# Moving the products of one chunk from GpSimd to VectorE, with three smaller changes of order, in a fused attention and FFN kernel

## The chip, the cores and the metric

The kernel runs on one core of a Trainium2 chip. Times are device microseconds (us) of one execution. A profile of one execution gives the "span", which is some 1.7 to 2.1 us shorter than the time, and the granted clock of TensorE. Engines: PE is TensorE, PEld its weight loads, DVE is VectorE, ACT is ScalarE, POOL is GpSimd, SP is SyncE. L392 is line 392 of the kernel profiled; from line 540 on the changed kernel's numbers are 6 or 7 lower than those of the kernel before.

## The reference

Attention with two kinds of local mask, then a gated FFN on its result:

```python
# q, k, v: 8 batches x 8 heads x 576 positions x 64, float32
scores = q @ k.T / 8
rel = pos[:, None] - pos[None, :]
mask_plain = (rel >= 0) & (rel < 32)                       # heads 0 to 3
mask_dil = (rel >= 0) & (rel < 128) & (rel % 4 == 0)       # heads 4 to 7
attn = softmax(where(mask, scores, -1e9)) @ v
x = attn.transpose(0, 2, 1, 3).reshape(4608, 512)
out = (gelu(x @ w_gate) * (x @ w_val)) @ w_out             # 512 -> 1536 -> 512
```

## The kernel before

The 4608 tokens go through the FFN in 9 chunks of 512. A chunk has 12 "ffn blocks" (128 gate and 128 value columns each, 8 matmuls) and then an "output phase" of four token blocks of 12 matmuls. Attention for later tokens is woven into the output phases. It goes by head pairs, numbered through all batches, four to a batch. Per pair: scores on TensorE, exponential on ScalarE, mask product on VectorE, sums and values on TensorE, then the divisors (a VectorE transpose out of PSUM, a reciprocal, a transpose back to `rb`) and the product with them into `xT`, the FFN's input.

In chunk 2 alone two of these products were given to GpSimd. GpSimd got them through a ScalarE copy `xc`:

```python
def norm_x(n, b0, flip=False, split=False):
    ...
        eng = nc.vector
        if split:
            xc = nrm.tile([P, 2, 2 * NCL], F32, tag="xc", bufs=1)
            nc.scalar.copy(xc, ps[:, b0 + flip : b0 + flip + 2, 0 : 2 * NCL])
            eng, num = nc.gpsimd, xc.rearrange("p s (m i) -> p i m s", m=2)
        eng.tensor_tensor(dst..., num, rb..., ALU.mult)
```

A string says where each piece stands in an output phase. "2.3v" means: in token block 2, before matmul 3, sums, values and divisors of the next pair; `s` is the scores of a further pair, `m` its mask product, `x` the product with the divisors on VectorE, `p` the same split over ScalarE and GpSimd, `w` a last pair in two parts.

```python
places = {
    1: "0.0m 1.3v 1.3s 1.3x 1.3m 2.5v 2.5s 2.5x 2.5m 3.0s 3.0m 3.6v 3.6x 3.12w",
    2: "0.0m 1.3v 1.3p 1.3s 1.3m 2.3v 2.3p 2.3s 2.3m 2.11s 3.0m 3.4s 3.5v 3.5x 3.12w 3.12m",
    ...
```

At the start, GpSimd's queue carries the q/k "eights", the last v rows (`vr`), and then the first weights `w0`; SyncE's queue carries the five parts of the v load (`sv`) and the dilated v load. `w0` is issued only when one part of `sv` has landed, the gate.

```python
qd0 = load_eights(0)
sv0 = new_v(0)
load_v_dil_rest(0)                      # vr
... identity and masks on GpSimd ...
gate_v = v_plain(0, sv0, nc.sync)       # returns the second part of sv
...
gate["dma"] = gate_v
load_w(0)
v_cast(0, sv0)
```

The softmax here doesn't subtract the row's maximum and nothing guards it: scores larger than these inputs give would overflow.

## Time and profile before

| | before |
|---|---|
| time, median of 3 | 352.05 us (351.19 to 352.19) |
| span of the profiled run | 350.2 us |
| TensorE busy | 336.9 us, 96% |
| stretch of chunk 2 | 24.06 us, of which TensorE idle 3.05 us |

The "stretch of chunk 2" runs from the first scores woven into its output phase to the second half of the third ffn block of chunk 3. The lines of the order in time are read so: the columns are start, duration, engine, line, operation, out<-in with shapes, and a count where equal neighbours are merged; the bracket tells how long the engine stood before it and what released it. This line, of the kernel before, ends the stretch:

```profile
144.78 0.59 PE L582 MATMUL ps<-xT,wv 128*128 128x512 f16 x2 [0.54 <-DVE u_all L605]
```

TensorE stood 0.54 us for a VectorE product of the first ffn blocks.

### The profile page before, as it was taken

Reading aid. Unit: us, or ns where it says so; the run is one execution under the profiler, and the core shown is the slowest. Engines: PE = TensorE matmul, PEld = TensorE weight load, DVE = VectorE, ACT = ScalarE, POOL = GpSimd, SP = SyncE. Lnnn points to the kernel's source line nnn. Section 1 sums busy time; section 2 is a strip of 40 time slices with the busy share of each in tenths; the row PEclk is TensorE's granted clock in tenths of the full one; section 3 lists DMA queues with packets and bytes.
Section 4 is the critical chain, followed back from the end, with each engine's and each line's share of the span. In section 5 each row is a group of like instructions: output and inputs, shape, how many; then the busy total and the mean of one; then the engine's idle time right before and its main releaser. Section 6 shows DMA issues by size and latency. Waiting matters only on the chain.

```text
span 350.2 us, 6012 instructions
## 1 busy us (share of the span) xinstructions
PE 336.9 (96%) x2342; PEld 163.8 (47%) x2342; DVE 202.3 (58%) x306; ACT 149.7 (43%) x223; POOL 86.4 (25%) x123
## 2 busy tenths in 40 slices
PE   8979989999999979999999999999999999999996
PEld 3644454444544444444454454444454444444444
DVE  3784488543793358783878666985399424303320
ACT  1853373435543537325553547326723223322321
POOL 8692404630630635063006300420000000000000
PEclk9999999999999999999999999999999999999999
DMA  8999999999999983999159953890200020021002
GB/s 180 227 197 230 201 184 186 186 160 266 179 149 227 173 157 69 229 151 140 63 156 178 135 112 113 190 151 32 90 2 0 32 90 1 2 79 41 2 30 90
DMA packets 106460, 44.44 MB, mean 127 GB/s; under 512 B 83296, under 2 KB 101856, under 8 KB 106432
## 3 DMA queue, kind: packets, MB, share of 16 engines
q1 hardware_dynamic: 84192, 31.01, 39.4%
q0 software_dynamic: 21696, 12.33, 27.2%
q10 hardware_dynamic: 544, 0.72, 0.8%
q8 instruction: 18, 0.29, 0.4%
q14 instruction: 10, 0.08, 0.1%
HBM read 39.85 MB, written 9.44 MB: 141 GB/s over the span
## 4 chain that ended last, share of the span: by engine, by line
PE 72%; DVE 10%; DMA 10%; issue 3%; ACT 2%; SPq 1%; POOL 1%; DVEq 0%; ACTq 0%; POOLq 0%
PE ps L582 42%; PE ps L616 22%; PE ps L464 4%; DMA st<-in_k_dram 4%; DMA sv<-in_v_dram 3%; DMA wv<-in_moe_w_val_dram 3%; DVE dt L492 2%; DVE u_all L605 2%; DVE P L392 2%; DVE dt L525 1%; DVE xT L502 1%; PE ps L352 1%; PE ps L382 1%; DVE rb L536 1%; PE ps L640 1%
## 5 line engine op out<-in xcount | busy, mean ns | idle before, releaser
L604 ACT ACTIVATE g<-ps 128x512 f16<-128x512 f32 x108 | 63.9, 597 | 123.7 <-PE ps L582 123.2
L605 DVE SCALAR_TENSOR_TENSOR u_all<-g,ps 128x512 f16<-128x512 f16 x108 | 72.8, 684 | 75.9 <-PE ps L582 67.9
L582 PE MATMUL ps<-xT,wv 128*128 128x512 f16 x432 | 113.8, 379 | 1.1 <-DMA wv<-in_moe_w_val_dram 0.6
L582 PE MATMUL ps<-xT,wg 128*128 128x512 f16 x432 | 114.2, 379 | 0.7 <-POOL xT L706 0.4
L616 PE MATMUL ps<-wo,u_all 128*128 128x512 f16 x420 | 97.2, 380 | 0.1
L582 PEld LDWEIGHTS <-wv 128*128 128x128 f16 x432 | 42.3, 98 | 53.4 <-issue 2.1
L582 PEld LDWEIGHTS <-wg 128*128 128x128 f16 x432 | 41.3, 98 | 48.6 <-issue 1.1
L616 PEld LDWEIGHTS <-u_all 128*128 128x128 f16 x420 | 38.4, 98 | 44.3 <-issue 0.7
L627 ACT ACTIVATE osb<-ps 128x512 f32<-128x512 f32 x33 | 19.7, 598 | 39.9 <-PE ps L616 39.9
L220 POOL CAST qp<-st 128x2048 f16<-128x2048 f32 x6 | 11.4, 1895 | 89.4 <-DMA st<-in_k_dram 71.8
L536 DVE STREAM_TRANSPOSE rb<-rc 128x576 f32<-128x576 f32 (+4 forms) x34 | 25.3, 743 | 1.4
L525 DVE STREAM_TRANSPOSE dt<-ps 128x576 f32<-128x576 f32 x21 | 16.4, 779 | 14.4 <-PE ps L464 14.2
L384 ACT ACTIVATE P<-ps 128x1152 f16<-128x1152 f32 x16 | 18.1, 1131 | 11.4 <-PE ps L382 11.1
L362 ACT ACTIVATE P<-ps 128x960 f16<-128x960 f32 x16 | 15.5, 972 | 7.1 <-PE ps L352 7.0
L392 DVE TENSOR_TENSOR P<-P,mask_d 128x1152 f16<-128x1152 f16 x13 | 11.5, 886 | 10.3 <-ACT P L384 10.3
L557 DVE TENSOR_TENSOR xT<-ps,rb 128x576 f16<-128x576 f32 x14 | 15.6, 1128 | 2.1 <-PE ps L464 1.9
L464 PE MATMUL ps<-P,ones 128*64 128x96 f16 (+5 forms) x174 | 11.2, 245 | 3.7 <-DVE P L392 3.3
L392 DVE TENSOR_TENSOR P<-P,mask_p 128x1344 f16<-128x1344 f16 x14 | 12.9, 939 | 3.3 <-ACT P L363 3.3
L464 PEld LDWEIGHTS <-ones 128*64 128x64 f16 x174 | 6.9, 109 | 13.0 <-issue 8.3
L629 DVE TENSOR_SCALAR osb<-ps 128x512 f32<-128x512 f32 x2 | 1.4, 692 | 18.2 <-PE ps L616 18.2
L247 POOL DMA_DIRECT2D vr<-in_v_dram x16 | 9.9, 628 | 7.3 <-DMA wv<-in_moe_w_val_dram 4.6
L204 POOL CAST vp<-sv 128x1024 f16<-128x1024 f32 x8 | 8.5, 1062 | 11.9 <-DMA sv<-in_v_dram 11.9
(88 smaller groups left out, 254.5 us busy)
## 6 DMA issues: line engine op xcount, KB each, us to landing
out_dram<-osb SPq DMA_DIRECT2D x35, 256.0 KB, 2.0
sv<-in_v_dram SPq DMA_DIRECT2D x40, 128.0 KB, 3.7
st<-in_q_dram SPq DMA_DIRECT2D x24, 128.0 KB, 3.7
st<-in_k_dram SPq DMA_DIRECT2D x24, 128.0 KB, 3.1
vd<-in_v_dram POOLq DMA_DIRECT2D x7, 256.0 KB, 7.1
wg<-in_moe_w_gate_dram POOLq DMA_DIRECT2D x3, 512.0 KB, 7.4
wv<-in_moe_w_val_dram POOLq DMA_DIRECT2D x3, 512.0 KB, 9.2
wo<-in_moe_w_out_dram POOLq DMA_DIRECT2D x3, 512.0 KB, 20.8
```

What stands on the lines that cost most here:

```text
L362: nc.scalar.activation(pt[:, :, 0:PB], sb[:, 0, :, 0:PB], AF.Exp, bias=0.0, scale=scale)
L384: nc.scalar.activation(pt, ps[:, b0 : b0 + 4, 0:DW], AF.Exp, bias=0.0, scale=scale)
L392: nc.vector.tensor_tensor(pt, pt, mb, ALU.mult)
L464: nc.tensor.matmul(o, lhs, rhs, start=st, stop=True, skip_group_check=True)
L525: nc.vector.transpose(dst, den)
L536: nc.vector.transpose(rb[:, 0 : 32 * nb].rearrange("p (b c) -> p b c", c=32), bass.AP(tensor=rc.tensor, offset=rc.offset, ap=[rc.ap[0], [1 ...
L557: eng.tensor_tensor(dst.rearrange("p (i m s) -> p i m s", m=2, s=2), num, rb.rearrange("p (s m i) -> p i m s", s=2, m=2), ALU.mult,)
L582: nc.tensor.matmul(ps[:, bank, :], w[:, kc, ns], xT[kc][:, tok], start=first, stop=end)
L604: nc.scalar.activation(g, ps[:, banks[0], :], AF.Gelu)
L605: nc.vector.scalar_tensor_tensor(u_all[:, nb, :], g, USCALE, ps[:, banks[1], :], ALU.mult, ALU.mult)
L616: nc.tensor.matmul(ps[:, bank, :], u_all[:, fc, tb * P : (tb + 1) * P], wo_t[fc // 4][:, fc % 4, :], start=(fc == 0), stop=(fc == NNB - 1),)
L627: nc.scalar.activation(osb, ps[:, bank, :], AF.Copy, bias=0.0, scale=1.0 / USCALE)
```

## The change

The intent: take the two products of chunk 2 back to VectorE and space its pieces as in chunk 1, since the GpSimd products and the VectorE masks got in each other's way; share the first casts differently between VectorE and ScalarE; let `w0` go as soon as the first part of `sv` is there. One mask product of chunk 0 also moves.

```diff
 def v_plain(b, sv, eng):
-            if kb == 1:
-                second = ins
-        return second
+            if kb == 0:
+                first = ins
+        return first
 def norm_x
-            if split: ... ScalarE copy, product on GpSimd ...
 first casts
-    for hp in range(2):
-        for t in range(2):
-            cast_six(("dve", "act")[t], q6, first_p, t, hp)
+    for t, hp, eng in ((0, 0, "dve"), (0, 1, "dve"), (1, 0, "act"), (1, 1, "dve")):
+        cast_six(eng, q6, first_p, t, hp)
 places
-        2: "0.0m 1.3v 1.3p 1.3s 1.3m 2.3v 2.3p 2.3s 2.3m 2.11s 3.0m 3.4s 3.5v 3.5x 3.12w 3.12m",
+        2: "0.0m 1.3v 1.3s 1.3x 1.3m 2.5v 2.5s 2.5x 2.5m 3.0s 3.0m 3.6v 3.6x 3.7s 3.12w 3.12m",
 chunk 0
             third(1, 0)
+            mask_next()
             den(4, 0)
-            mask_next()
```

More of the change, by code (lines that the diff above doesn't have):

```diff
@@ L540, in recip, with norm_x @@
         tiles["rb", n] = rb
-    def norm_x(n, b0, flip=False, split=False):
+    def norm_x(n, b0, flip=False):
         b = n // NHP
@@ L551, in norm_x @@
             num = ps[:, b0 + flip : b0 + flip + 2, 0 : 2 * NCL].rearrange("p s (m i) -> p i m s", m=2)
-            eng = nc.vector
-            if split:
-                xc = nrm.tile([P, 2, 2 * NCL], F32, tag="xc", bufs=1)
-                nc.scalar.copy(xc, ps[:, b0 + flip : b0 + flip + 2, 0 : 2 * NCL])
-                eng, num = nc.gpsimd, xc.rearrange("p s (m i) -> p i m s", m=2)
-            eng.tensor_tensor(
+            nc.vector.tensor_tensor(
                 dst.rearrange("p (i m s) -> p i m s", m=2, s=2),
@@ L868, in do @@
                     mask_next()
-                elif kind in "xp":
-                    norm_x(*going.pop(0), split=kind == "p")
+                elif kind == "x":
+                    norm_x(*going.pop(0))
                 elif kind == "v":
```

## The prediction

In rival (a) the words cut said that the masks' losses, 1.5 and 1.2 us (2.28 against 0.76, 2.86 against 1.65), would go away. No term of the sum is cut; it came to 352.05 - 2.4 - 0.3 - 0 + 0.4 = 349.75. The 2.4 rests on the times of chunk 1 (0.76 us for the mask, 1.13 us for the product). The 0.4 is an estimate from the packets counted in the trace: 157 on GpSimd's queue and 157 on SyncE's from 9 to 10 us, then 208 and 205, and 261 and 269 in the two microseconds after. "Full" in it means that the 16 DMA engines were busy for 90% or more of every slice of 1.5 us from 3 to 51 us.

> **What bounds the kernel now.** First the page: the span, the busy shares and the chain that ended last.
>
> ```profile
> span 350.2 us, 6012 instructions
> ...
> PE 336.9 (96%) x2342; PEld 163.8 (47%) x2342; DVE 202.3 (58%) x306; ACT 149.7 (43%) x223; POOL 86.4 (25%) x123
> ...
> PE 72%; DVE 10%; DMA 10%; issue 3%; ACT 2%; SPq 1%; POOL 1%; DVEq 0%; ACTq 0%; POOLq 0%
> ```
>
> TensorE works nearly throughout, so only places where it stands can give time. A step counts if it moves the moment at which TensorE goes on. I looked next at the stretch from the first scores of a chunk's output phase to the second half of the third ffn block of the next chunk, for chunks 1, 2 and 3.
>
> ```profile
> core 0: us, PE busy (x) PEld busy (x) DVE busy (x) ACT busy (x) POOL busy (x), PEclk, DMA share, GB/s
> 83.31:104.22 20.91, 20.45 (x198) 10.32 (x197) 15.48 (x26) 10.96 (x15) 8.84 (x12) 1.00 1.13 165
> 120.72:144.78 24.06, 21.01 (x204) 10.44 (x204) 17.33 (x26) 13.74 (x20) 7.60 (x8) 1.00 0.79 143
> 161.86:181.73 19.87, 19.67 (x183) 9.78 (x183) 13.79 (x20) 12.31 (x17) 0.73 (x2) 1.00 0.46 104
> ```
>
> Chunk 2 has 3.05 us of idle TensorE (24.06 less 21.01), the others 0.46 and 0.20. Its order of instructions in time says why:
>
> ```profile
> 126.07 0.64 ACT L555 COPY xc<-ps 128x576 f32<-128x576 f32 x1 [1.59 <-DVE dt L525]
> 127.31 2.13 POOL L557 TENSOR_TENSOR xT<-xc,rb 128x576 f16<-128x576 f32 x1 [1.05 <-DVE rb L536]
> 127.78 2.28 DVE L392 TENSOR_TENSOR P<-P,mask_d 128x1152 f16<-128x1152 f16 x1 [0.62 <-ACT P L384]
> 130.11 0.44 PE L464 MATMUL ps<-P,ones 128*64 128x192 f16 x8 [1.90 <-DVE P L392]
> 133.76 2.86 DVE L392 TENSOR_TENSOR P<-P,mask_p 128x1344 f16<-128x1344 f16 x2 [0.90 <-ACT P L363]
> ```
>
> The mask product took 2.28 us; the same form took 0.76 us in chunk 1. It ends 0.62 us after GpSimd's product (127.31 + 2.13 = 129.44). The second GpSimd product stretches the two plain masks to 2.86 us, against 1.65 us in chunk 1. The ScalarE copy also holds the exponential until 126.61, though its scores were finished at 125.51.
>
> The start, where parts two and three act:
>
> ```profile
> 11.93 0.78 POOL L139 DMA_DIRECT2D wg<-in_moe_w_gate_dram  x1 [1.36 <-DMA sv<-in_v_dram]
> 15.04 1.04 POOL L204 CAST vp<-sv 128x1024 f16<-128x1024 f32 x1 [1.59 <-DMA sv<-in_v_dram]
> 18.19 1.06 POOL L293 CAST vd<-st 128x1024 f16<-128x1024 f32 x1
> 20.66 0.38 PE L582 MATMUL ps<-xT,wg 128*128 128x512 f16 x1 [0.37 <-POOL xT L706]
> 21.64 0.39 PE L582 MATMUL ps<-xT,wv 128*128 128x512 f16 x1 [0.60 <-DMA wv<-in_moe_w_val_dram]
> 41.52 0.43 PE L306 MATMUL ps<-ident,qp 96*128 96x96 f16 x6 [0.57 <-POOL qp L293]
> ```
>
> The last line is the key one. TensorE finishes six transposes at about 40.79 (40.53 + 6 x 0.043) and stands until 41.52, for a cast of a k load that landed at 40.6. The DMA engines are full from 2 to 50 us, so whatever TensorE gains earlier than this is lost here, and up to 0.73 us of delay is absorbed here.
>
> [...] The plain product from PSUM takes 0.76 us; the dilated one, with its reordered access, takes 1.13 us, and I use that. [...] From 9 to 10 us, with 1024-byte packets on the GpSimd queue and mostly 256-byte ones on the SyncE queue[...]:
>
> ```profile
> q0 software_dynamic: 157, 0.15, 91.7%
> q1 hardware_dynamic: 157, 0.04, 33.2%
> ```
>
> **Part 1, chunk 2.** Removed: two ScalarE copies (0.64 us) and two GpSimd products (2.13 us). Added: two VectorE products of 1.13 us. Chunk 1 has this schedule already, so I lay its intervals over chunk 2. Nothing moves up to the sums of head pair 12, at 124.43. Scores 13 then end at 125.45, and 14 ffn matmuls (0.216 us each) end at 128.5. VectorE: transposes and reciprocal end at 127.16 as now, product 127.2 to 128.33, mask 13 to about 129.05. So pair 13 starts at 129.1 instead of 130.11: 1.0 us. Chunk 1's intervals then give (offset from pair 13's start): the following mask done 4.7 us later, pair 14 at 133.85. Now it is 136.42, since scores 15 and 16 both stand before it and wait for the exponentials; the change moves scores 16 behind it. From pair 14 the VectorE chain is unchanged: divisors and product 3.5 us, the last pair in two parts 3.4 us, mask 16 0.85 us, the first ffn product 0.65 us. It ends at 142.25 and TensorE's third ffn block goes on at 142.35 instead of 144.78. Gain 2.4 us, with 1.9 to 2.8 possible. Idle left: 0.6 us before pair 13, 0.5 before pair 14, 0.7 before the third ffn block. TensorE runs on from there and the next batch's data land at 129.0 and 163.1, well before their scores (134.8 and about 170), so the gain stays.
>
> **Part 2, chunk 0's masks.** The diff also moves one mask product ahead of a divisor:
>
> ```profile
> 51.16 0.82 DVE L392 TENSOR_TENSOR P<-P,mask_p 128x1344 f16<-128x1344 f16 x1
> 52.02 0.48 PE L464 MATMUL ps<-P,ones 128*64 128x512 f16 x6 [0.58 <-DVE P L392]
> ```
>
> The exponential for that mask is done at 49.14, so it can run 49.2 to 50.0, and the sums start at 51.3 instead of 52.02. VectorE's total there is the same, though: the next divisor's read still ends at 53.4, and the next sums overwrite those banks, so they start at 53.45 instead of 53.77. Gain 0.3 us.
>
> **Part 3, first casts.** ScalarE has two casts of 0.83 us (8.44 to 10.01), VectorE two of 0.60 us (to 8.89). After: ScalarE one, VectorE three, to about 9.45. TensorE's warm-up runs to 9.2 and its 24 transposes follow without a break but for 0.08 us at 9.94, which waited for the second k cast. The bias product moves to 9.95, still before TensorE wants it at 10.3. Gain 0.1 us, then lost at the q/k load of 13.15 that TensorE already waits for, and again at 41.52: 0.
>
> **Part 4, the gate.** The first v part landed at 9.38, the second at 11.64. GpSimd finishes its masks at 10.56, so w0 is issued at about 10.6 instead of 11.93. Can it help? wv landed at 21.60, and TensorE waited at 21.64. But the fourth weight step waits for VectorE's product of pair 3, done at 24.1, and TensorE now stands only 0.1 us there. So earlier weights give nothing behind 24.1. They can hurt: their packets (98 ns each) take turns with the last v parts and the dilated v load on the SyncE queue. w0's packets appear about 2 us after issue, so from about 12.9 instead of 14.3. Between 13 and 16 the SyncE queue must still move about 600 packets of 256 bytes and 500 of 1024. Sharing at the 9-to-10 rate (157 a microsecond, against 563 from 13 to 14 beside only the tail of the other loads) I estimate the cast at 15.04 0.5 to 1 us later and the one at 18.19 1 to 1.5 us later; all that follows on GpSimd slips, and the first ffn block ends 0 to 1.7 us later, 1.1 as a middle. The stop at 41.52 absorbs 0.73. Cost 0.4 us, between 0 and 1.
>
> Sum: 352.05 - 2.4 - 0.3 - 0 + 0.4 = 349.75.
>
> **Rivals.** (a) VectorE becomes the bound in chunk 2, since it gets 2.3 us more while it already carries 17.33 us in the stretch: for it, 0.6 us of new waiting before pair 13; against it, [...]chunk 1 runs this order with 0.46 us idle. It would leave a gain of about 1 us in part 1: 352.05 - 1 - 0.3 + 0.4, so 351.1. (b) The gate costs its full 1.5 us or more, with a hole in the weight queue that moves the load landing at 40.6: 352.05 - 2.7 + 1.5, so 350.9. For it, DMA shares near full; against it, total bytes do not change. (c) The gate costs nothing, as the v loads are nearly through by 13: 349.3, the sum without the 0.4. (d) The gate helps the start: only if the load landing at 40.6 moved forward, against a full DMA: 348.8 with half a microsecond of it.
>
> **Range and chances.** Chunk 2 carries the change; its spread is 0.5 us each way, the start's about 0.5. Runs of the kernel before spread over 1 us. I say 349.7, between 348.7 and 350.9. 2% is 7 us, more than all idle time touched here: within 2% almost surely.
>
> **What would show it.** No ScalarE copy and no GpSimd product in chunk 2, mask 13 at about 0.76 us, pair 13 at 4.65 us after pair 12's start, and the stretch at 21.6 us instead of 24.06. In chunk 0 the wait at 52.02 gone and 0.3 us at most kept. At the start w0's issue at 10.6, the v cast and dilated-v cast later than 15.04 and 18.19, and the wait at 41.52 smaller or gone. I am wrong if the chunk 2 stretch stays above 23 us, if the casts come no later, or if the k load moves from 40.6.

## The result, and the profile after

Four runs of each kernel on one chip: 349.15 us median after (349.05 to 349.6) against 351.66 before (351.19 to 352.19). Ratios in this text are the mean time of one kernel's fast runs over the mean of the other's of the same rounds, so not quite the ratio of the medians quoted; here 0.9931, with a 95% interval of 0.9911 to 0.995. That is 2.4 us, within 2%, and within the range predicted.

The page of the changed kernel:

```profile
span 347.3 us, 6004 instructions
...
PE 335.7 (97%) x2342; PEld 163.3 (47%) x2342; DVE 202.1 (58%) x309; ACT 147.9 (43%) x220; POOL 82.2 (24%) x121
...
PE 71%; DVE 12%; DMA 10%; issue 3%; ACT 2%; POOL 1%; SPq 1%; DVEq 0%; POOLq 0%; ACTq 0%
```

VectorE was given two products more and yet was busy no longer (202.1 against 202.3 us): the products took 1.14 us each, but the masks of pairs 13 to 15 took 2.42 us instead of 5.14, and the page counts all of that as busy. The same three stretches, chunks 1, 2 and 3, with the columns as in the prediction:

```profile
82.73:103.66 20.93, 20.46 (x198) 10.32 (x198) 15.51 (x26) 10.96 (x15) 8.85 (x12) 1.00 1.22 174
120.16:141.88 21.72, 20.50 (x204) 10.46 (x203) 16.80 (x28) 12.33 (x18) 3.08 (x5) 1.00 0.69 135
158.97:178.84 19.87, 19.68 (x184) 9.78 (x184) 13.80 (x20) 12.30 (x17) 0.00 (x0) 1.00 0.48 108
```

Chunk 2 went from 24.06 to 21.72 us, chunks 1 and 3 kept theirs. The order in time in chunk 2:

```profile
126.63 1.14 DVE L551 TENSOR_TENSOR xT<-ps,rb 128x576 f16<-128x576 f32 x1
127.69 0.75 DVE L392 TENSOR_TENSOR P<-P,mask_d 128x1152 f16<-128x1152 f16 x1
128.49 0.44 PE L464 MATMUL ps<-P,ones 128*64 128x192 f16 x8 [0.41 <-DVE P L392]
132.32 1.67 DVE L392 TENSOR_TENSOR P<-P,mask_p 128x1344 f16<-128x1344 f16 x2
133.24 0.49 PE L464 MATMUL ps<-P,ones 128*64 128x64 f16 x10 [0.22 <-DVE P L392]
141.88 1.02 PE L576 MATMUL ps<-xT,wv 128*128 128x512 f16 x4 [0.23 <-DVE u_all L599]
```

The mask of pair 13 takes 0.75 us (before 2.28), the two plain masks 1.67 (before 2.86), and TensorE's wait for the mask of pair 13 falls from 1.90 to 0.41 us. Pair 14 starts 4.75 us after pair 13, with a wait of 0.22 us. The line that ends the stretch waits 0.23 us instead of 0.54.

Chunk 0, where the mask moved:

```profile
49.07 0.86 DVE L392 TENSOR_TENSOR P<-P,mask_p 128x1344 f16<-128x1344 f16 x1 [0.66 <-ACT P L363]
51.27 0.48 PE L464 MATMUL ps<-P,ones 128*64 128x512 f16 x6
```

The sums no longer wait. And the start:

```profile
10.76 0.78 POOL L139 DMA_DIRECT2D wg<-in_moe_w_gate_dram  x1
15.25 1.04 POOL L204 CAST vp<-sv 128x1024 f16<-128x1024 f32 x1 [2.96 <-DMA sv<-in_v_dram]
21.84 0.39 PE L576 MATMUL ps<-xT,wv 128*128 128x512 f16 x1 [0.59 <-DMA wv<-in_moe_w_val_dram]
41.42 0.43 PE L306 MATMUL ps<-ident,qp 96*128 96x96 f16 x6 [0.26 <-POOL qp L293]
```

`w0` is issued 1.17 us earlier (10.76 against 11.93), but the v cast (before 15.04) and TensorE's wait for the value weights (before 21.64) are no earlier.

**Where the 2.9 us of span went.** The kernel can be split at four moments that every profile has. The first is the stop at 41.4 (six transposes that wait for the next batch's k), the second the first ffn matmul of chunk 1, the third the first scores of chunk 2's output phase, the fourth the end of the stretch.

| us | start to the stop | stop to chunk 1 | to chunk 2's scores | stretch of chunk 2 | to the end | span |
|---|---|---|---|---|---|---|
| before | 41.52 | 20.96 | 58.24 | 24.06 | 205.44 | 350.22 |
| after | 41.42 | 20.49 | 58.25 | 21.72 | 205.44 | 347.32 |
| difference | 0.10 | 0.47 | -0.01 | 2.34 | 0 | 2.90 |

In three later profiles (chunk2_back, only_mask, only_casts) the k load had landed by 40.0 us and TensorE passed the stop without a wait, so the stop does not always absorb what happens before it.

So three questions were put to the chip. Does each part do what this table says when it stands alone? What in chunk 2 made the gain: the engine, or the places? And why did an earlier issue of `w0` move nothing?

### The profile page after: what moved, and what is told of

It reads as the page before. It is cut to its first block, busy times and chain, and to the rows that moved or that the text cites. A ratio compares the mean times of both kernels' runs of the same rounds, so it can differ in the third digit from the quotient of the medians.

```text
span 347.3 us, 6004 instructions
## 1 busy us (share of the span) xinstructions
PE 335.7 (97%) x2342; PEld 163.3 (47%) x2342; DVE 202.1 (58%) x309; ACT 147.9 (43%) x220; POOL 82.2 (24%) x121
## 4 chain that ended last, share of the span: by engine, by line
PE 71%; DVE 12%; DMA 10%; issue 3%; ACT 2%; POOL 1%; SPq 1%; DVEq 0%; POOLq 0%; ACTq 0%
PE ps L576 42%; PE ps L610 21%; PE ps L464 4%; DMA st<-in_k_dram 4%; DMA sv<-in_v_dram 3%; DMA wv<-in_moe_w_val_dram 3%; DVE dt L492 2%; DVE u_all L599 2%; DVE dt L525 2%; DVE rb L536 1%; DVE P L392 1%; DVE xT L551 1%; DVE xT L502 1%; PE ps L382 1%; PE ps L352 1%
## 5 line engine op out<-in xcount | busy, mean ns | idle before, releaser
L551 DVE TENSOR_TENSOR xT<-ps,rb 128x576 f16<-128x576 f32 x16 | 17.9, 1131 | 2.2 <-PE ps L464 1.9
L392 DVE TENSOR_TENSOR P<-P,mask_d 128x1152 f16<-128x1152 f16 x13 | 9.8, 750 | 9.7 <-ACT P L384 9.7
L392 DVE TENSOR_TENSOR P<-P,mask_p 128x1344 f16<-128x1344 f16 x14 | 11.8, 856 | 2.9 <-ACT P L363 2.9
L492 DVE STREAM_TRANSPOSE dt<-ps 64x576 f32<-64x576 f32 x14 | 10.9, 781 | 0.4
```

Of the source, the lines that this page charges most:

```text
L392: nc.vector.tensor_tensor(pt, pt, mb, ALU.mult)
L492: nc.vector.transpose(dt[64 * hl : 64 * hl + 64].rearrange("p b c -> p (b c)"), both_rows(1 - hl, b0, hl))
L551: nc.vector.tensor_tensor(dst.rearrange("p (i m s) -> p i m s", m=2, s=2), num, rb.rearrange("p (s m i) -> p i m s", s=2, m=2), ALU.mult,)
```

## The experiments

Each group of runs has its own rounds of the kernel before.

### Each part alone

Kernel before in these rounds: 351.51 us median of 11 runs (350.91 to 353.2).

**chunk2_back**: the changed kernel with the split products and the old places of chunk 2, that is, the other three parts alone.

```diff
+ norm_x with split as before
-        2: "0.0m 1.3v 1.3s 1.3x 1.3m 2.5v 2.5s 2.5x 2.5m 3.0s ... (new)
+        2: "0.0m 1.3v 1.3p 1.3s 1.3m 2.3v 2.3p 2.3s 2.3m 2.11s ... (old)
```

> The changed kernel with chunk 2 alone as it was before (split products on ScalarE and GpSimd, old places). My theory: chunk 2 carries 2.3 to 2.4 us, the rest about 0.5, so this is 0.3 to 0.6 us faster than before (about 351.3 against 351.7 to 352.0) and the stretch from the first scores of chunk 2 to the third ffn block's second half is back at 24.06 us. Rival (the gain is the start's, or the parts help each other): over 1 us faster than before.

**only_mask**: the kernel before with the mask of chunk 0 moved.

```diff
             third(1, 0)
+            mask_next()
             den(4, 0)
-            mask_next()
```

> Before, with only the mask product of chunk 0 moved ahead of the divisor. My theory: the sums that started at 52.02 start at about 51.3, the next ones at 53.2 to 53.5, so 0.3 to 0.6 us faster. Rival: the 0.57 us seen at the end of chunk 0 came from the k load's landing and other chance at the start; then 0.1 us or less here.

**only_gate**: the kernel before with the gate of `w0` on the first part of `sv`.

```diff
-            if kb == 1:
-                second = ins
-        return second
+            if kb == 0:
+                first = ins
+        return first
```

> Before, with only the gate of w0 on the first v part. As I predicted before the change ran: v casts 0.5 to 1.5 us later than 15.04 and 18.19, first ffn block later by about 1 us, 0 to 1 us slower in all. New theory from the changed kernel's trace (w0 lands no earlier though it is issued 1.2 us earlier): w0 issued at about 10.6, landing at 21.6 to 21.8, v casts within 0.3 us of before, total within 0.2 us of before.

**only_casts**: the kernel before with the first casts shared anew.

```diff
-            cast_six(("dve", "act")[t], q6, first_p, t, hp)      # for hp, for t
+    for t, hp, eng in ((0, 0, "dve"), (0, 1, "dve"), (1, 0, "act"), (1, 1, "dve")):
+        cast_six(eng, q6, first_p, t, hp)
```

> Before, with only the three casts on VectorE. Theory: the first scores 0.1 to 0.2 us earlier, nothing left of it at the wait for k's cast near 41.5 us, total within 0.2 us of before. Rival: the start's gain survives, 0.2 us or more faster.

Measured:

| | time, median (range) | ratio to before, 95% | to the stop | stop to chunk 1 | stretch of chunk 2 |
|---|---|---|---|---|---|
| chunk2_back | 351.41 (350.5 to 351.9) | 0.9986 (0.9965 to 1.0007) | 40.84 | 20.48 | 24.05 |
| only_mask | 350.91 (350.06 to 351.89) | 0.9978 (0.9955 to 1.0002) | 40.83 | 20.48 | 23.38 |
| only_gate | 352.32 (351.91 to 353.12) | 1.0017 (0.9996 to 1.0039) | 41.45 | 20.96 | 24.05 |
| only_casts | 352.31 (351.14 to 353.11) | 1.001 (0.9986 to 1.0035) | 40.93 | 20.96 | 25.66 |

None of the four times can be told from the kernel before; all ratio intervals hold 1, so the times neither confirm nor refute the gains of 0.3 to 0.6 us that were expected of chunk2_back and only_mask. One expectation was missed: in only_casts the first scores came at 11.26 us, later than the 10.99 of the kernel before and not 0.1 to 0.2 us earlier. The stages of the table tell more than the times. With the moved mask the interval from the stop to chunk 1 is 20.48 or 20.49 us, without it 20.96; the same holds in every later profile. So this part is worth 0.48 us. The gate and the casts touch neither interval.

The stretch of chunk 2 is another matter: with its old code it took 24.06, 24.05 and 24.05 us, but 23.38 in only_mask and 25.66 in only_casts, and neither edit touches chunk 2. In the order in time of only_mask, GpSimd and VectorE show why:

```profile
126.61 1.23 POOL L260 COPY kTr<-qTd 128x512 f16<-128x512 f16 x1 [4.48 <-DMA qTd<-rd]
126.61 0.76 DVE L392 TENSOR_TENSOR P<-P,mask_d 128x1152 f16<-128x1152 f16 x1 [0.63 <-ACT P L384]
```

Here a copy of keys, which waits for a load, came up on GpSimd just as the mask of pair 13 began. The mask took its short 0.76 us, and the copy took 1.23 us instead of its usual 0.61. GpSimd's product came behind both. In only_casts GpSimd's product is first, by 0.06 us (by 0.47 us in the kernel before, chunk2_back and only_gate), and an earlier mask in the same stretch had already taken 1.38 us instead of 0.76 beside the casts of v on GpSimd:

```profile
127.16 2.12 POOL L557 TENSOR_TENSOR xT<-xc,rb 128x576 f16<-128x576 f32 x1
127.22 2.69 DVE L392 TENSOR_TENSOR P<-P,mask_d 128x1152 f16<-128x1152 f16 x1 [0.62 <-ACT P L384]
```

That is only the first 0.4 of the 1.6 us that only_casts lost in this stretch (25.66 against 24.06). TensorE stood 2.30 us for the mask of pair 13 there, against 1.90 in the kernel before, chunk2_back and only_gate. Then, from 130.22 to 133.64 us, the granted clock was 0.50, which the stretch of no other profile here shows:

```profile
129.96 0.48 PE L464 MATMUL ps<-P,ones 128*64 128x192 f16 x8 [2.30 <-DVE P L392]
131.55 2.91 PE L616 MATMUL ps<-wo,u_all 128*128 128x512 f16 x8
```

The eight output matmuls of the last line took 1.90 us in the kernel before. Some 0.8 us more was lost by the end of the half clock, and the last 0.4 us at the third ffn block, behind a gap of 0.47 us on VectorE whose cause the trace does not show. That the longer wait brought the half clock on is not shown: it is one profile, and no run varied the wait alone.

So the old chunk 2 was not just slow but uneven: which of the two engines started first differed between these profiles, and in only_mask it was a copy waiting for a load until 126.61 us that put GpSimd's product last. With VectorE's products at the new places it took 21.72 in three profiles (after, and two runs below). The spread of the times agrees: the kernel before ranges over 2.3 us in these rounds, the changed kernel over 0.55 us in its four runs. Part of that spread goes with the clock: of the 53 runs of the experiments that had the old code of chunk 2, 13 have a mean clock of 0.994 or 0.995 and a median of 352.91 us, the other 40 one of 351.56. None of the 36 runs with any other code of chunk 2 is under 0.998.

### What in chunk 2 made the gain

Kernel before in these rounds: 351.91 us median of 7 runs (351.22 to 352.39). The expectations of this group count the stretch from the first ffn matmul of chunk 2, 21.37 to 21.38 us earlier: there it is 45.43 us for the kernel before and 43.10 for the changed kernel. In that count the four runs came to 44.13 (lock_read), 43.10 (lock_memset), 42.89 (new_places_gpsimd) and 43.47 (old_places_vectore). The first case of old_places_vectore is the one in which GpSimd's products beside the masks are most of the loss. lock_memset asks whether GpSimd's work lengthens the mask when it only writes.

**lock_read**: the changed kernel, with one GpSimd product that reads SBUF put back beside the mask of pair 13. Its result is used by nobody.

```diff
         tiles["rb", n] = rb
+        if n == 12:
+            xc = nrm.tile([P, 2, S], F16, tag="xc", bufs=1)
+            twice = bass.AP(tensor=rb.tensor, offset=rb.offset, ap=[rb.ap[0], [0, 2], [1, S]])
+            nc.gpsimd.tensor_tensor(xc, twice, twice, ALU.mult)
```

> The changed kernel plus one useless GpSimd product (two SBUF reads, 128x1152, about 2.8 us) that starts when the divisors of head pair 12 are ready, so it runs beside the mask product of pair 13. Theory[...]: that mask product takes 0.75 us plus the rest of GpSimd's, 2 to 2.7 us in all, ends about 0.65 us after GpSimd's, and pair 13 starts 1 to 2 us later than in the changed kernel; the stretch grows by as much from 43.10 (first ffn matmul of chunk 2 to the third block's second half in chunk 3). Rival (the copy on ScalarE and the places were the cost[...]): the mask stays at 0.75 us and nothing moves.

**lock_memset**: the same place, but three GpSimd memsets, which write SBUF and read nothing.

```diff
-        nc.vector.transpose(
+        last = nc.vector.transpose(
         ...
         tiles["rb", n] = rb
+        if n == 12:
+            xc = nrm.tile([P, 2 * S], F16, tag="xc", bufs=1)
+            for i in range(3):
+                ins = nc.gpsimd.memset(xc, 0.0)
+                if i == 0:
+                    tc.add_manual_dep(ins.ins, last.ins.name, SYNC, reason="at the same time")
```

> As the run with the useless product, but GpSimd only writes: three memsets of 128x1152 f16 in a row (about 1 us each), started by the same divisors. Theory[...]: the mask stays at 0.75 us and the stretch at 43.1 us. Rival (any GpSimd work blocks it): the mask takes 1 to 1.8 us.

lock_read first, then lock_memset:

```profile
126.39 2.10 POOL L544 TENSOR_TENSOR xc<-rb 128x1152 f16<-128x1152 f32 x1 [0.67 <-DVE rb L536]
127.41 1.70 DVE L392 TENSOR_TENSOR P<-P,mask_d 128x1152 f16<-128x1152 f16 x1
```

```profile
127.23 3.29 POOL L544 MEMSET xc<- 128x1152 f16 x3
127.94 0.76 DVE L392 TENSOR_TENSOR P<-P,mask_d 128x1152 f16<-128x1152 f16 x1
```

Beside the product that reads, the mask takes 1.70 us and ends 0.62 us after it (128.49 and 129.11). That is the same 0.62 us as in the kernel before. The expected 2 to 2.7 us were missed because the product was done in 2.10 us, not 2.8, and pair 13 started just under 1 us later than in the changed kernel (a wait of 1.37 us instead of 0.41). Beside the memsets, which cover it wholly, it takes 0.76 us. The stretch is 22.76 us with the reading product and 21.72 with the memsets (time 349.88 and 349.26, one run each). So in these two runs the mask lost 0.95 us beside a GpSimd product that reads SBUF (1.70 against 0.75 in the changed kernel) and 0.01 us beside memsets that only write it. What the two engines contend for is not shown. The product of VectorE that ran beside lock_read's GpSimd product, with one input in PSUM, kept its 1.14 us.

**new_places_gpsimd**: the kernel before with the new places, the products still split over ScalarE and GpSimd.

```diff
-        2: "0.0m 1.3v 1.3p 1.3s 1.3m 2.3v 2.3p 2.3s 2.3m 2.11s 3.0m 3.4s 3.5v 3.5x 3.12w 3.12m",
+        2: "0.0m 1.3v 1.3s 1.3p 1.3m 2.5v 2.5s 2.5p 2.5m 3.0s 3.0m 3.6v 3.6x 3.7s 3.12w 3.12m",
```

> Before, with only the places of chunk 2 as in the changed kernel; the products stay split over ScalarE and GpSimd. If the new places carry the gain[...]: the exponential of pair 13 comes ahead of the ScalarE copy, the mask is ready before GpSimd's product starts[...], stretch 42.6 to 43.5 us (before 45.43, changed 43.10). If GpSimd's products are themselves the cost: 44.5 us or more.

**old_places_vectore**: the kernel before with the products on VectorE, at the old places.

```diff
-        2: "0.0m 1.3v 1.3p 1.3s 1.3m 2.3v 2.3p 2.3s 2.3m ...
+        2: "0.0m 1.3v 1.3x 1.3s 1.3m 2.3v 2.3x 2.3s 2.3m ...
```

> Before, with only the engine of chunk 2's products changed to VectorE, at the old places. [...]both masks back at 0.75 and 1.7 us, stretch 43.3 to 44.3 us, between before's 45.43 and the changed kernel's 43.10, the rest being the scores of pair 16 that still stand ahead of pair 14. If the places are most of it: 44.5 us or more.

| | time, median (range) | ratio to before, 95% | stretch of chunk 2 |
|---|---|---|---|
| new_places_gpsimd | 349.5 (348.71 to 349.83) | 0.9932 (0.9916 to 0.9949) | 21.51 |
| old_places_vectore | 349.74 (349.54 to 350.0) | 0.9936 (0.9922 to 0.9951) | 22.10 |

Either half alone brings most of the gain or all of it: 2.55 and 1.96 us of the stretch against 2.34 for both. They don't add: both shorten the mask of pair 13 (2.28 us before, 0.72 and 0.75 here) and with it TensorE's wait for that mask (1.90 us before, none and 0.84 here). In new_places_gpsimd:

```profile
126.37 0.72 DVE L392 TENSOR_TENSOR P<-P,mask_d 128x1152 f16<-128x1152 f16 x1
126.60 2.51 POOL L557 TENSOR_TENSOR xT<-xc,rb 128x576 f16<-128x576 f32 x1 [0.94 <-ACT xc L555]
127.87 0.44 PE L464 MATMUL ps<-P,ones 128*64 128x192 f16 x8
```

The scores of pair 13 stand ahead of the product now, so on ScalarE the exponential runs before the copy `xc`. The exponential starts 4.84 us into the stretch instead of 5.89. The mask is ready when VectorE comes to it and starts 0.23 us before GpSimd's product; now it is GpSimd that is late (2.51 us instead of 2.13), and nobody waits for it. TensorE starts pair 13 without a wait. That is better than the changed kernel does here (0.41 us wait), since VectorE is spared 1.1 us of product ahead of the mask. With VectorE's products the mask comes later, but in the changed kernel no instruction of GpSimd stands beside it (none ran from 125.0 to 136 us) and it took 0.75 us. In old_places_vectore TensorE waits 0.84 us for the mask of pair 13, in the changed kernel 0.41 us; the places account for that difference.

### Where an early w0 is held, and two candidates

Kernel before in these rounds: 352.31 us median of 11 runs (350.67 to 353.96).

First the packets, counted from the trace's packet records: `w0` and the eights move in packets of 1024 bytes, `vr` in 512 packets of 256 bytes, all on GpSimd's queue.

| us | w0 issued | last packet of the eights | last packet of vr | first packet of w0 | first half of w0 landed | v cast |
|---|---|---|---|---|---|---|
| before | 11.93 | 12.72 | 14.33 | 13.91 | 19.04 | 15.04 |
| only_casts | 12.18 | 12.48 | 14.10 | 14.14 | 19.15 | 15.07 |
| only_gate | 10.62 | 12.38 | 14.00 | 13.70 | 19.08 | 14.83 |
| after | 10.76 | 12.65 | 14.27 | 14.15 | 19.23 | 15.25 |

In all four, issued from 10.62 to 12.18, `w0` starts as `vr` ends: its first packet came between 0.42 us before the last one of `vr` and 0.04 us after it. That led to the last question.

**w0_ahead**: the changed kernel with `vr` issued behind the first half of `w0`.

```diff
     sv0 = new_v(0)
-    load_v_dil_rest(0)
 def load_w(i):
+    both = []
+    for t, w in ((wg_t, moe_w_gate), (wv_t, moe_w_val)):
+        both.append(nc.gpsimd.dma_start(out=t[i], in_=w[:, cs].rearrange("(kc p) n -> p kc n", p=P)))
+        if i == 0 and len(both) == 1:
+            load_v_dil_rest(0)
```

> The changed kernel, with the two loads of the last v rows (issued on the GpSimd queue at the very start, 256-byte packets) put behind the first half of w0, so that w0 has no queued load ahead of it but the q/k eights. In the changed kernel w0 was issued 1.17 us earlier than before, yet its 1024-byte packets began at 14.0 in both, just when the 256-byte packets of those v rows ran out. Theory Q (what held w0 was the queue in front of it, not the gate): w0's packets now begin at about 12.5 us, when the packets of the q/k eights end, and the first half of w0 lands 1 to 1.5 us before 19.23. Rival L (packets begin a fixed time of some 3 us after the issue, whatever is queued): they still begin at about 13.8 to 14. On the cost that my prediction gave to an early w0 (sharing with the v loads on the SyncE queue): if that mechanism exists, the v cast moves from 15.25 to 15.7 or later and the dilated v cast from 18.39 to 18.8 or later; if it does not, both stay within 0.3 us. The last v rows land later, at 16 to 17, which may hold the first dilated values by a few tenths. Time 349.2 to 349.8 in each case, since the stop at 41.4 absorbs most of it.

Measured: 348.98 us (348.64 to 349.2, 4 runs), ratio 0.9906 (0.9874 to 0.9937); the order in time of GpSimd:

```profile
10.66 0.79 POOL L140 DMA_DIRECT2D wg<-in_moe_w_gate_dram  x1 [1.43 <-DMA sv<-in_v_dram]
14.19 1.04 POOL L205 CAST vp<-sv 128x1024 f16<-128x1024 f32 x1 [0.76 <-DMA sv<-in_v_dram]
```

The first packet of `w0` came at 13.39 and its first half landed at 18.25, 0.98 us before that of the changed kernel. So the loads ahead in the queue were holding it: with `vr` out of the way its first packet came 0.76 us earlier. But 13.39 is not the 12.5 that I expected when nothing but the eights is ahead: they ended at 12.76, and 0.63 us followed without a packet of `w0`. What filled these 0.63 us is not shown. The rival, a fixed delay of about 3 us from the issue, falls as well: the delay is 2.7 us here, 3.4 us in the changed kernel and 2.0 us in only_casts.

The v cast did not come later but 1.06 us earlier, at 14.19, and the dilated cast 17.33 instead of 18.39. SyncE's 256-byte packets ended at 13.92 instead of 14.88, once `vr` was out of the way. That fits loads of the two queues slowing each other, with `vr` as the one that slowed the v loads (in the changed kernel 223 packets of GpSimd's queue and 228 of SyncE's from 10 to 11 us, 251 and 250 from 11 to 12); `w0`, which began at 13.39, hardly ran beside them. And all of this is worth nothing in the end: the first two ffn blocks, which run together, ended at 25.17 (25.20 in the changed kernel) and the stop came at 41.18.

How far the stop moves by itself: in the 13 other profiles it came at 40.84 to 41.70 us in the six with the new gate (mean 41.35), and at 40.81 to 41.80 in the seven with the old one (mean 41.23). A part of the change that acts at the start would have to be worth well over half a microsecond to be seen.

**mask16_later**: the changed kernel with the mask of pair 16 put behind the first two ffn products of chunk 3, which it stood ahead of; its result is wanted only at the fifth ffn block of chunk 3.

```diff
-        2: "... 3.6v 3.6x 3.7s 3.12w 3.12m",
+        2: "... 3.6v 3.6x 3.7s 3.12w",
-        masks = []
+        masks = masks if c == 3 else []
 in the loop over ffn blocks
+            if c == 3 and nb == 1:
+                masks.pop(0)()
-            while masks:
+            while masks and c != 2:
                 mask_next()
```

> The changed kernel, with the mask product of head pair 16 taken from the end of chunk 2 (where it stands 0.85 us ahead of the first two ffn products of chunk 3 on VectorE) and put behind those two; its result is wanted only 4 ffn blocks later. If VectorE's chain is what the third ffn block waits for (0.23 us idle in the changed kernel), the wait goes and the stretch of chunk 2 shrinks from 21.72 to about 21.5: time 0.2 to 0.3 us under the changed kernel, so 348.9, span 347.0. If the wait is for something else, nothing changes.

**gpsimd_and_mask**: new_places_gpsimd with the mask order of chunk 0 (edit as in only_mask).

> The kernel before with two of the change's parts in another form: the new places in chunk 2 but the two products left on GpSimd (with their ScalarE copies), and the mask order of chunk 0. No new casts, no new gate. If the two gains add, 1.9 to 2.6 us of chunk 2 (the run with the new places alone) and 0.48 us of chunk 0: time about 349.0, span 346.5, that is level with or 0.2 us below the changed kernel. If the gain of the places alone depends on a race that falls differently from run to run, mask 13 takes 2 us or more in the trace and the time is near 351.

**gpsimd_mask16**: gpsimd_and_mask with the mask of pair 16 later as well (edit as in mask16_later).

> The run gpsimd_and_mask with the mask product of pair 16 put behind the first two ffn products of chunk 3 as well. In the run with the new places and GpSimd products the third ffn block stood 0.54 us for VectorE; this should go: time about 348.5, span 346.0, the best of all. If the mask only shifts the wait to a later block, it is level with gpsimd_and_mask.

| | time, median (range), 6 runs | ratio to before, 95% | to the stop | stop to chunk 1 | stretch of chunk 2 | span |
|---|---|---|---|---|---|---|
| mask16_later | 348.61 (348.28 to 348.75) | 0.9895 (0.987 to 0.9921) | 41.53 | 20.48 | 21.33 | 347.0 |
| gpsimd_and_mask | 349.26 (348.95 to 350.12) | 0.9914 (0.9886 to 0.9943) | 41.80 | 20.49 | 22.08 | 348.0 |
| gpsimd_mask16 | 348.92 (348.05 to 350.88) | 0.9909 (0.9877 to 0.994) | 41.43 | 20.48 | 20.86 | 346.4 |

In mask16_later the mask fills a gap that VectorE has anyway, and TensorE goes on without a wait:

```profile
140.72 1.28 DVE L599 SCALAR_TENSOR_TENSOR u_all<-g,ps 128x512 f16<-128x512 f16 x2
141.92 0.85 DVE L392 TENSOR_TENSOR P<-P,mask_p 128x1344 f16<-128x1344 f16 x1
```

The stretch is 21.33 us, 0.39 less than with the changed kernel's code, where about 0.2 was expected, and the time 348.61 where 348.9 was. It was not run in one set of rounds with the changed kernel; the nearest comparison is w0_ahead of the same rounds, which has the changed kernel's chunk 2 (stretch 21.72) and took 348.98, so 0.37 us more. mask16_later is faster than the kernel before for certain. That it beats the changed kernel by 0.4 us rests on the stretch and on that comparison.

gpsimd_mask16 has the shortest stretch (20.86) and the single fastest run of all (348.05), but it ranges to 350.88. Its sibling gpsimd_and_mask shows how that can come about. In its profiled run, its slowest of six, GpSimd's casts of v fell beside the first mask of the stretch, which took 1.14 us instead of 0.76. The key copy, which waits for a load, came 3.2 us later in the stretch than in new_places_gpsimd and the first product behind it 2.3 us later, and another mask took 1.21 us, 0.82 in new_places_gpsimd:

```profile
129.39 2.17 POOL L557 TENSOR_TENSOR xT<-xc,rb 128x576 f16<-128x576 f32 x1
131.06 1.21 DVE L392 TENSOR_TENSOR P<-P,mask_p 128x1344 f16<-128x1344 f16 x1
```

The stretch was 22.08 there, against 21.51 with the same places in new_places_gpsimd. The race expected at mask 13 did not come up (it took 0.72 us); it came up at other masks. Expected were a time of 349.0 and a span of 346.5; the median came out at 349.26. For gpsimd_mask16 they were 348.5 and 346.0, against 348.92 and 346.4. How often each order comes up over many runs I have not counted. A product on GpSimd can fall beside a mask again (1.21 us for the mask above, beside a product of 2.17); on VectorE it took 1.08 to 1.16 us in all 16 cases of the changed kernel.

## Why the prediction was right

The time, 349.15 us, lies 0.55 us under the 349.7 predicted and inside the range. By its steps:

- **Part 1, chunk 2: right in size and by its own steps.** Predicted were pair 13 at 129.1, pair 14 4.75 us later, and the end at 142.35, on the clock of the kernel before. The changed kernel's stretch began 0.56 us earlier, so on that clock it measured 129.05, 4.75 and 142.44. The gain was 2.34 us, 2.4 predicted. The idle left was smaller in places (0.41, 0.22 and 0.23 us against 0.6, 0.5 and 0.7), made up for by one of 0.25 us before pair 15 that had not been named. What the prediction did not see is that either the engine or the places would have done.
- **Part 2, mask order: the mechanism right, the size off.** The term mis-sized was the next sums, put at 53.45, held by the next divisor's read that "still ends at 53.4". In the trace they started at 53.20 (53.30 on the clock of the kernel before), since the divisor chain moved up too, and 0.48 us was kept instead of 0.3.
- **Part 3, casts: right that nothing is kept; the 0.1 us before that is not shown.** only_casts left every interval but the uneven chunk 2 as it was. The first scores came at 10.86 in the changed kernel instead of 10.99, but over all 14 profiles they came at 10.47 to 11.26 with the new casts and at 10.54 to 11.30 with the old ones, so that agreement is no more than chance.
- **Part 4, the gate: this step failed.** "w0's packets appear about 2 us after issue, so from about 12.9 instead of 14.3" is what did not happen. They waited behind `vr` in GpSimd's own queue and began at 14.15; the casts that were to come 0.5 to 1.5 us later moved by 0.2 us, no more than between runs. So the cost of 0.4 us was not there. Rival (c), 349.3, had the right number, but by luck: its reason was that the v loads are nearly through by 13, and SyncE's 256-byte packets ended only at 14.88. That loads of two queues slow each other, which I had estimated from the 157 and 157 packets, fits w0_ahead, where the v cast moved by 1.06 us, but I charged it to a load that was not yet running. The prediction had itself named what would refute it: that the casts come no later.

The two errors, 0.4 us of cost that did not exist and 0.2 us of gain too few, point the same way. Together they are the 0.6 us by which the difference of the two profiles (2.90) exceeds the forecast of 2.3. The times do not show this excess: they say 2.4 us (1.8 to 3.1 by the interval), and 0.39 of the 0.55 us between 349.15 and 349.7 is the kernel before, which ran at 351.66 in these rounds and not at 352.05. That the forecast gain and the timed one lie so near is in part luck. Rivals (a), (b) and (d) are refuted: the stretch was 21.72 and not above 23; the casts did not slip; and the k load landed at 40.48 against 40.59, a difference much smaller than that load's variation of 39.88 to 40.87 over the other profiles.

That GpSimd's product was what stretched the mask had not been shown when the prediction was made; only the runs show it, by lock_read (1.70 us), lock_memset (0.76 us) and new_places_gpsimd (0.72 us for the mask that started first, 2.51 for GpSimd's product). And that `w0` would stand behind `vr` on its own queue, as the four rows of packets show, I had not thought of.

## What to carry to other kernels

When a VectorE operation takes three times its usual time (here 2.28 us instead of 0.76), look for what GpSimd started just before it (here a product, 0.47 us before). Either move the work or change the order so that the operation that others wait for starts first; an order that depends on when loads land came here with an uneven stretch (23.38 to 25.66 us), so prefer the one that cannot collide (21.72 us in three profiles). An earlier issue of a load moved next to nothing here (1.3 us earlier, first packet 0.2 us) while other loads stood ahead of it in the same queue: find its first packet, not its issue. And split the span at a few moments that every profile has: here that showed 0.48 us in each of nine profiles, where five rounds of timing showed nothing. Look at the granted clock over time too, and not at its mean alone: in only_casts 0.995 was 3.4 us at half clock.

## Some figures that the traces gave

- Six dilated v loads of the changed kernel that were issued from GpSimd with no packet of its queue in the 2 us before had their first packet 1.50, 1.80, 2.40, 2.55, 2.56 and 3.13 us after the start of the issue, which itself took 0.76 to 0.77 us. `w0` took 2.0 to 3.4 us with loads ahead of it.
- 1.3 us of earlier issue of `w0` (10.62 against 11.93) moved the first packet by 0.2 us (13.70 against 13.91), while taking two loads out of the way moved it by 0.76 us (14.15 to 13.39).
- The plain product of 576 columns, which reads one input from PSUM, took 0.72 to 0.76 us (5 of them in the kernel before); the same size in a reordered pattern took 1.09 to 1.16 us (14 of them).
- The mask of 1152 columns ended 0.62 us after GpSimd's product in the kernel before and in lock_read, less than its 0.76 us alone.
